# An attention and two-layer feed-forward kernel on one core: value matmuls one item later, weight conversions spread out, PSUM copies divided by size

## The chip, the cores and the metric

The kernel runs on one core of one Trainium2 chip. The metric is the device time of one execution in microseconds. Before the change the median of three runs is 1132.71 us (1131.9 to 1133.64). One further execution was profiled; where the text gives a time of a single instruction, it is from that one.

## The reference

Inputs are `q`, `k`, `v` of 4 batches x 8 heads x 576 positions x 64 in fp32, and four float64 weight matrices (512x2048, 2048x512, twice). What is computed, cut to its core:

```python
q_rot, k_rot = rotate(q), rotate(k)                  # rotary embedding, halves of 32
scores = matmul(q_rot, k_rot.T) / sqrt(64)
attn = exp(scores - max(scores)); attn = attn / (sum(attn) + 1e-9)
x = (attn @ v)   -> 2304 tokens x 512
h = x @ w_in;  g = where(h > 0, h, exp(min(h, 0)) - 1);  x = g @ w_out      # first feed-forward
h = x @ w_in2; g = h - tanh(h);                          out = g @ w_out2   # second
```

## The kernel before

**Attention.** The 32 heads are worked on as 16 pairs. A pair has nine *items*: four blocks of 128 queries for each of its two heads (numbers 0 to 7, the heads in turn) and item 8, which holds the last 64 queries of both. The main loop runs over the 144 items of all pairs, `for i in range(n + D + 1)`, and in iteration i it issues, in this order: the row maximum of item i (`emit_max`, L220, VectorE), the score matmuls of item i+1 (`emit_s`, L211, into one of two PSUM tiles `s`), the exponential of item i (`emit_exp`, L234, ScalarE), the PSUM copies that the iteration before left over (`flush`), the division by the row sum (`emit_norm`, GpSimd), preparation steps of a later pair (`prep`, five steps for each of q and k: two products and a sum for the rotation, a rounded copy, a remainder, then DMAs that put the halves in place), one part of a weight conversion, the transposes of item i-4 (`emit_t`, L291, and the small `pr` ones, into one of three PSUM tiles), and the value matmuls that are due (`emit_pv`, L325).

All engines take their instructions strictly in this order; nothing is reordered at run time. So the place of an instruction in its engine's row decides what stands behind it when it waits. The score tile of item i+2 reuses that of item i, and so waits for the exponential of item i. `flush` deals its copies out in turn: of five, two go to VectorE and three to ScalarE, large (`aT`, 512 columns) or small (`aTr`, up to 128 columns) alike. `PV_AT` says how many iterations after the last transpose of a group its value matmuls are issued: chunks 0 to 2 one later, 3 and 4 three later (the small last group: two).

**Weights.** A weight block (128 x 512, float64) is loaded by `load_w` and turned into two fp32r halves by `conv_w` in NCV = 5 parts: ScalarE `Abs` (L83), two VectorE operations together (L85, L86), one (L90), one (L94), and at the end a ScalarE copy (L102) with a GpSimd subtraction (L103). The work tile `f` has one buffer, so a conversion can't begin until the GpSimd subtraction of the one before it has read `f`. Eight blocks, `first_w`, are converted in attention, one in 18 items.

**Feed-forward.** 192 steps (layer, group of 512 hidden units, one of six blocks of 384 tokens, one of four 128-wide slices). Step i issues `emit_f1(i)` (L445: 12 matmuls), the split of a slice of the next token block's input into two halves (`split_x`: ScalarE copy L54, GpSimd subtraction L55), the split of step i-2's result (`emit_split`), the activation (`emit_act`, L456), its VectorE part (`emit_dve`), conversion parts, and `emit_f2(i-4)` (L503). The four slices of token block 1 are split in steps 0 to 3, and `emit_f1(4)` reads all four.

Of the kernel before, what the change touches and what calls it, by code (L numbers as in the profile page):

```python
# [23 lines left out]
def attention_elu_tanhshrink(ctx: ExitStack, tc: tile.TileContext, qk, v, w1i, w1o, w2i, w2o, tab, out):  # L24
# [14 lines left out]
    NG, NJ = 4, 4  # L39
# [28 lines left out]
        raw_t[key] = t  # L68

    cv_t = {}  # L70
    NCV = 5

    def conv_w(key, slot, part):
        l, kind, c = key
        if part < 4:
            words = raw_t[key].bitcast(U32).rearrange("p (n t) -> p n t", t=2)
            lo_w, hi_w = words[:, :, 0], words[:, :, 1]
        if part == 0:
            cv_t[key] = cv_p.tile([128, 512], F32, tag="f", name="f")
        f = cv_t[key]  # L80
        fu = f.bitcast(U32)
        if part == 0:
            nc.scalar.activation(out=f, in_=hi_w.bitcast(F32), func=AF.Abs)  # L83
        elif part == 1:
            nc.vector.tensor_scalar(out=f, in0=f, scalar1=LO_CLAMP, scalar2=HI_CLAMP, op0=ALU.max, op1=ALU.min)  # L85
            nc.vector.tensor_scalar(  # L86
                out=fu, in0=fu, scalar1=3, scalar2=0x3FFFFFFF, op0=ALU.logical_shift_left, op1=ALU.bitwise_and
            )
        elif part == 2:
            nc.vector.scalar_tensor_tensor(  # L90
                out=fu, in0=hi_w, scalar=0xC0000000, in1=fu, op0=ALU.bitwise_and, op1=ALU.bitwise_or
            )
        elif part == 3:
            nc.vector.scalar_tensor_tensor(  # L94
                out=fu, in0=lo_w, scalar=29, in1=fu, op0=ALU.logical_shift_right, op1=ALU.bitwise_or
            )
            raw_t.pop(key)
        else:
            w = w_pools[slot // 4 if slot < 4 else -1].tile(
                [128, 2, 512], F32R, tag=f"w{kind}_{slot}", name=f"w{kind}_{slot}"  # L100
            )
            nc.scalar.copy(out=w[:, 0, :], in_=f)  # L102
            nc.gpsimd.tensor_tensor(out=w[:, 1, :], in0=f, in1=w[:, 0, :].bitcast(F32), op=ALU.subtract)  # L103
            w_t[key] = w
            cv_t.pop(key)


    with ExitStack() as actx:
# [143 lines left out]
                    out=a, in0=a, scalar1=r[:, x:x + 1], scalar2=1.0, op0=ALU.mult, op1=ALU.mult  # L252
                )

        ev = [0]
        late, late_x = [], []

        def evac(out_, in_):
# [1 line left out]

        def flush():
            for out_, in_ in late:
                ev[0] += 1
                if ev[0] % 5 in (1, 3):
                    nc.vector.tensor_copy(out_, in_)  # L265
                else:
                    nc.scalar.copy(out_, in_)  # L267
            late.clear()
            for p, grp, o, n in late_x:
                b, hp = divmod(p, 4)  # L270
                x0 = NTOK * hp + b * S + 256 * grp
                nc.scalar.copy(out=xa[:, x0:x0 + n], in_=o[:, 0:n])
            late_x.clear()
# [60 lines left out]
        D = 4  # L334
        NDIRECT = 2
        NI = 9
        first_w = [(0, kind, c) for c in range(NJ) for kind in range(2)]
        sched = {}
        early = {1: ((None, 0, 0, 1, 2, 3), (None, 0, 0, 0, 1, 2)), 2: ((0, 4, 5, 7, 7, 8), (4, 7, 9, 11, 12, 13))}
        for p in range(1, NPAIR):  # L340
            i0 = NI * (p - 1)
            for x in range(2):
                when = [i0 + o for o in ((-10, -6, -4, -3, -2, -1), (-7, -2, 0, 2, 3, 4))[x]]
                if p in early:
                    when = early[p][x]
                if when[0] is not None:
                    sched.setdefault(when[0], []).append((load_qk, p, x))
                for k in range(5):
                    sched.setdefault(when[k + 1], []).append((prep, p, x, k))
            sched.setdefault(i0 + 7, []).append((load_v, p))  # L350
        with tc.manual_schedule():
# [17 lines left out]
                prep(0, 1, i)  # L369
            n = len(items)  # L370
            pend = []
            nw = list(range(len(first_w)))[::-1]
            emit_s(0)
            PV_AT = ((1, 1, 1, 3, 3), (1, 1, 1, 3, 3), (2, 2, 2, 2, 2))
            for i in range(3, 5):
                for x in range(2):
                    prep(0, x, i)
            for i in range(n + D + 1):
                p, r = divmod(i, NI)
                for f, *arg in sched.get(i, ()):  # L380
                    if f is not prep:
                        f(*arg)
                if i == 1 or i % (2 * NI) == 12:
                    load_w(first_w[nw.pop()]) if nw else None
                if i < n:
                    emit_max(i)
                if i + 1 < n:
                    emit_s(i + 1)
                if i < n:
                    emit_exp(i)  # L390
                flush()
                if 0 <= i - 1 < n:
                    emit_norm(i - 1)
                if p < NPAIR:
                    for f, *arg in sched.get(i, ()):
                        if f is prep:
                            f(*arg)
                    c = NI * (p % 2) + r - 3
                    if c >= 0 and c % 2 == 0 and c // 2 < NCV and p // 2 < len(first_w):
                        key = first_w[p // 2]  # L400
                        conv_w(key, key[2], c // 2)
                if 0 <= i - D < n:
                    emit_t(i - D)
                    pp, uu, hh = items[i - D]
                    if uu in (1, 3) and hh == 1 or uu == 4:
                        for c in range(5):
                            pend.append((i + PV_AT[uu // 2][c], pp, uu // 2, c))
                for x in [x for x in pend if x[0] <= i]:
                    emit_pv(*x[1:])
                    pend.remove(x)  # L410
                if n - 8 <= i < n and (i - n) % 2 == 0:
                    split_x(0, (i - n + 8) // 2)
# [115 lines left out]
                    nc.sync.dma_start(out=out[128 * r:128 * r + 128, :], in_=a)  # L528

    y_done = []  # L530
    conv = [(l, kind, NJ * g + j) for l in range(2) for g in range(NG) for j in range(NJ) for kind in range(2)]
    conv = conv[2 * NJ:]
    LAG = 4
    with tc.manual_schedule():
        nc.vector.memset(b1, B1)
# [3 lines left out]
        todo = [(key, part) for key in conv for part in range(NCV)]  # L539
        nload = ndone = 0  # L540
        for i in range(n + LAG + 1):
            if i < n:
                emit_f1(i)
            emit_acc()
            if i < NJ * (NT - 1):
                split_x(i // NJ + 1, i % NJ)
            if 0 <= i - 2 < n:
                emit_split(i - 2)
            if i < n:
                emit_act(i)  # L550
            if 0 <= i - 1 < n:
                emit_dve(i - 1)
            while nload < len(conv) and nload <= i // 3:
                load_w(conv[nload])
                nload += 1
            while ndone < len(todo) and ndone < (i - 2) * NCV // 3:
                key, part = todo[ndone]
                ndone += 1
                conv_w(key, key[2] % NJ + NJ * ((key[0] * NG + key[2] // NJ) % 2), part)
            if 0 <= i - LAG < n:  # L560
                emit_f2(i - LAG)
# [57 lines left out]
```

## Time and profile before

| what | value |
|---|---|
| median of the runs | 1132.71 us |
| profiled execution | 1132.65 us, of it the span 1130.9 us |
| TensorE matmul busy | 1097.3 us (97%) |
| VectorE busy | 765.6 us (68%) |
| ScalarE busy | 688.6 us (61%) |
| GpSimd busy | 671.3 us (59%) |

The span falls into a start up to about 24 us, attention up to about 319 us, and feed-forward after it. Engines in rows: PE is TensorE's matmul, PEld its weight load, DVE is VectorE, ACT ScalarE, POOL GpSimd, SP the engine that issues the DMAs. A matmul's row can be longer than its share of the engine, since matmuls overlap; the distance of starts tells the pace. A name before the arrow is written, those behind it are read.

### The profile page before, as it was taken

To read this page: it belongs to the slowest core of one execution; us is meant where nothing else is said; L and a number is where in the kernel's file an instruction comes from. 1 tells how busy PE (TensorE), PEld (TensorE's weight loads), DVE (VectorE), ACT (ScalarE), POOL (GpSimd) and SP (SyncE) were. 2 spreads that over 40 slices of the span, in tenths; PEclk is the share of its full clock that TensorE was granted. 3 is DMA by queue.
4 is the path that set the end of the run, shared out by engine and by line. 5 is a ranking of instruction groups with operands and counts; after the bars stand their busy time and mean duration, and the time that the engine had idled before them with its cause. 6 is when DMAs were issued, how large, how long until landed. Compare 5 with 4: busy or idle time off the path is not lost.

```text
span 1130.9 us, 18518 instructions
## 1 busy us (share of the span) xinstructions
PE 1097.3 (97%) x6656; PEld 987.2 (87%) x6656; DVE 765.6 (68%) x1393; ACT 688.6 (61%) x1477; POOL 671.3 (59%) x609
## 2 busy tenths in 40 slices
PE   2899999999999999999999999999999999999998
PEld 2777776777799999999999999998998899899987
DVE  6988888888645434555545556678768877877665
ACT  3676766676745533333333344688888788877774
POOL 2877887887556533333333466676666666666443
PEclk9999999999999999999999999999999999999999
DMA  7767676865211111112111121111111111110102
GB/s 232 217 193 200 181 215 169 222 172 164 72 39 38 40 55 38 38 38 55 40 38 38 38 57 38 39 38 38 57 38 38 38 56 38 38 39 1 57 35 78
DMA packets 29627, 91.96 MB, mean 81 GB/s; under 512 B 4192, under 2 KB 4192, under 8 KB 29536
## 3 DMA queue, kind: packets, MB, share of 16 engines
q1 hardware_dynamic: 29536, 90.78, 28.3%
q8 instruction: 53, 0.87, 0.3%
q14 instruction: 38, 0.31, 0.1%
HBM read 57.74 MB, written 4.72 MB: 55 GB/s over the span
## 4 chain that ended last, share of the span: by engine, by line
PE 90%; DVE 5%; DMA 2%; ACT 2%; SPq 1%; issue 1%; ACTq 0%; DVEq 0%
PE h L445 36%; PE y L503 18%; PE y L505 17%; PE o L325 8%; PE s L211 6%; PE pt L291 4%; DVE nm L220 2%; DMA k<-hl 1%; ACT a L234 1%; DVE t L148 1%; DVE aT L265 1%; ACT aT L267 1%; DVE hl L156 0%; DMA tabs<-in_tab 0%; PE pr L304 0%
## 5 line engine op out<-in xcount | busy, mean ns | idle before, releaser
L445 PE MATMUL h<-x,w 128*128 128x384 f32 x2304 | 434.0, 336 | 0.0
L445 PEld LDWEIGHTS h<-x,w 128*128 128x128 f32 x2304 | 407.1, 188 | 8.0 <-ACT a L234 0.4
L488 POOL TENSOR_TENSOR g<-f,g 128x384 fp32r<-128x384 f32 x192 | 213.6, 1113 | 187.8 <-ACT g L487 182.5
L503 PE MATMUL y<-g,w 128*128 128x384 f32 x1152 | 219.0, 339 | 0.0
L505 PE MATMUL y<-w,g 128*128 128x512 f32 x864 | 216.7, 395 | 0.2 <-ACT xa L520 0.2
L503 PEld LDWEIGHTS y<-g,w 128*128 128x128 f32 x1152 | 204.0, 188 | 0.0
L505 PEld LDWEIGHTS y<-w,g 128*128 128x128 f32 x864 | 161.5, 188 | 31.9 <-ACT xa L520 0.6
L251 POOL TENSOR_SCALAR a<-a,r 128x576 f32<-128x576 f32 x144 | 135.2, 951 | 63.7 <-DVE r L248 43.6
L464 POOL TENSOR_TENSOR w<-w,u 128x384 f32<-128x384 f32 x96 | 105.4, 1098 | 99.7 <-ACT w L463 99.7
L234 ACT ACTIVATE a<-s,nm 128x576 f32<-128x576 f32 x144 | 107.1, 743 | 89.6 <-DVE nm L220 75.1
L487 ACT CAST g<-f 128x384 fp32r<-128x384 f32 x192 | 98.0, 510 | 94.1 <-PE y L503 92.4
L475 DVE TENSOR_SCALAR f<-f 128x384 f32<-128x384 f32 x96 | 40.0, 416 | 145.4 <-ACT f L456 145.4
L456 ACT ACTIVATE f<-h 128x384 f32<-128x384 f32 x96 | 47.2, 492 | 146.7 <-PE h L445 143.8
L220 DVE TENSOR_REDUCE nm<-s 128x1 f32<-128x576 f32 x144 | 108.2, 753 | 38.1 <-PE s L211 36.5
L103 POOL TENSOR_TENSOR w<-f,w 128x512 fp32r<-128x512 f32 x64 | 82.6, 1291 | 54.4 <-ACT w L102 54.3
L522 DVE TENSOR_TENSOR xa<-y,xa 128x384 f32<-128x384 f32 (+1 forms) x126 | 74.0, 612 | 47.3 <-PE y L503 42.0
L479 DVE TENSOR_TENSOR f<-h,f 128x384 f32<-128x384 f32 x96 | 53.1, 553 | 68.3 <-ACT f L465 67.8
L481 DVE COPY_PREDICATED f<-mask,w 128x384 f32<-128x384 uint32 x96 | 92.2, 961 | 10.3 <-DVE w L480 0.5
L325 PE MATMUL o<-aT,v 128*64 128x256 f32 (+1 forms) x768 | 89.3, 339 | 2.6 <-ACT aT L267 2.4
L146 POOL TENSOR_TENSOR t<-t,tabs 128x576 f32<-128x576 f32 x59 | 86.3, 1463 | 8.2 <-DMA t<-in_qk 8.2
L291 PE MATMUL pt<-ident,a 128*128 128x128 f32 x576 | 88.3, 277 | 0.1
L461 ACT ACTIVATE u<-h 128x384 f32<-128x384 f32 x96 | 47.4, 494 | 66.4 <-PE h L445 52.1
(55 smaller groups left out, 1379.2 us busy)
## 6 DMA issues: line engine op xcount, KB each, us to landing
k<-hl SPq DMA_DIRECT2D x64, 288.0 KB, 4.2
t<-in_qk SPq DMA_DIRECT2D x30, 576.0 KB, 6.2
raw<-in_w1i SPq DMA_DIRECT2D x16, 512.0 KB, 3.7
raw<-in_w1o SPq DMA_DIRECT2D x16, 512.0 KB, 3.7
raw<-in_w2i SPq DMA_DIRECT2D x16, 512.0 KB, 3.6
raw<-in_w2o SPq DMA_DIRECT2D x16, 512.0 KB, 3.6
v<-in_v SPq DMA_DIRECT2D x16, 288.0 KB, 4.7
qa<-hl SPq DMA_DIRECT2D x32, 144.0 KB, 4.0
```

What stands on the lines that cost most here:

```text
L220: nc.vector.tensor_reduce(out=nm, in_=s_t[i][:, :, 0:288], axis=AX.XY, op=ALU.max, negate=True)
L234: nc.scalar.activation(out=a.rearrange("p (x c) -> p x c", x=2), in_=s[:, :, 0:288], func=AF.Exp, bias=nm_t.pop(i), scale=1.0, accum_out=den,)
L251: nc.gpsimd.tensor_scalar(out=a, in0=a, scalar1=r[:, x:x + 1], scalar2=1.0, op0=ALU.mult, op1=ALU.mult)
L291: nc.tensor.transpose(pt[:, c, :], a[:, h or 0, c0:c0 + 128], ident)
L325: nc.tensor.matmul(out=o[sl, 0:n], lhsT=w, rhs=m, start=(c == 0), stop=(c == 4))
L445: nc.tensor.matmul(out=hp, lhsT=w[:, wp, ws], rhs=x_t[t][:, xp, c, :], start=(m == 0), stop=(m == 3 * KC - 1))
L464: nc.gpsimd.tensor_tensor(out=w, in0=w, in1=u, op=ALU.mult)
L481: nc.vector.copy_predicated(f, mask.bitcast(U32), w)
L487: nc.scalar.copy(out=g[:, 0, :], in_=f)
L488: nc.gpsimd.tensor_tensor(out=g[:, 1, :], in0=f, in1=g[:, 0, :].bitcast(F32), op=ALU.subtract)
L503: nc.tensor.matmul(out=y_t[e][:, 0:NB], lhsT=w[:, wp, es], rhs=gt[:, gp, :], start=st, stop=sp)
L505: nc.tensor.matmul(out=y_t[e], lhsT=gt[:, gp, es], rhs=w[:, wp, :], start=st, stop=sp)
```

## The change

Three things change. The value matmuls are due one iteration later (`PV_AT`). `flush` gives every copy of at most 128 columns to VectorE and every larger one to ScalarE. The weight conversions are cut into NCV = 6 parts (L85 and L86 apart) and spread: one block takes 28 items, with its parts at offsets `CV_AT`, so that five blocks (`NFIRST`) instead of eight are converted in attention; the other three, which are the `w_out` blocks of the first group's slices 1 to 3, are converted whole in steps 0, 1 and 2 of feed-forward, and their loads stand on SP's queue behind attention's last. Preparation steps move by up to one iteration. From step 3 on, feed-forward converts one block in three steps, as before.

```diff
-    NCV = 5
+    NCV = 6
...
         elif part == 1:
             nc.vector.tensor_scalar(out=f, in0=f, scalar1=LO_CLAMP, scalar2=HI_CLAMP, op0=ALU.max, op1=ALU.min)
+        elif part == 2:
             nc.vector.tensor_scalar(
                 out=fu, in0=fu, scalar1=3, scalar2=0x3FFFFFFF, op0=ALU.logical_shift_left, op1=ALU.bitwise_and
             )
...
+    conv = [(0, kind, c) for kind in range(2) for c in range(NJ)]
+    conv += [(l, kind, NJ * g + j) for l in range(2) for g in range(NG) for j in range(NJ) for kind in range(2)][2 * NJ:]
+    NFIRST = NJ + 1
...
         def flush():
             for out_, in_ in late:
-                ev[0] += 1
-                if ev[0] % 5 in (1, 3):
+                if out_.free_size() <= 128:
                     nc.vector.tensor_copy(out_, in_)
                 else:
                     nc.scalar.copy(out_, in_)
...
-        first_w = [(0, kind, c) for c in range(NJ) for kind in range(2)]
+        CYC, CV_AT = 28, (5, 8, 12, 17, 21, 24)
...
-                when = [i0 + o for o in ((-10, -6, -4, -3, -2, -1), (-7, -2, 0, 2, 3, 4))[x]]
+                when = [i0 + o for o in ((-10, -7, -6, -4, -3, -2), (-7, -2, -1, 1, 2, 3))[x]]
...
-            PV_AT = ((1, 1, 1, 3, 3), (1, 1, 1, 3, 3), (2, 2, 2, 2, 2))
+            PV_AT = ((2, 2, 2, 4, 4), (2, 2, 2, 4, 4), (3, 3, 3, 3, 3))
...
-                if i == 1 or i % (2 * NI) == 12:
-                    load_w(first_w[nw.pop()]) if nw else None
+                key, at = divmod(i, CYC)
+                key = conv[key] if key < NFIRST else None
+                if key and at == 0:
+                    load_w(key)
...
-                    c = NI * (p % 2) + r - 3
-                    if c >= 0 and c % 2 == 0 and c // 2 < NCV and p // 2 < len(first_w):
-                        key = first_w[p // 2]
-                        conv_w(key, key[2], c // 2)
+                    if key and at in CV_AT:
+                        conv_w(key, key[2], CV_AT.index(at))
...
-    conv = conv[2 * NJ:]
+    conv = conv[NFIRST:]
...
-            while nload < len(conv) and nload <= i // 3:
-                load_w(conv[nload])
-                nload += 1
-            while ndone < len(todo) and ndone < (i - 2) * NCV // 3:
+            upto = NCV * min(i + 1, 2 * NJ - NFIRST) + max(0, (i - 2) * NCV // 3)
+            while ndone < min(len(todo), upto):
+                while nload < len(conv) and nload <= ndone // NCV + 1:
+                    load_w(conv[nload])
+                    nload += 1
                 key, part = todo[ndone]
```

On TensorE, around item 8 of the first full pair (the `s` row with 224 columns belongs to it), the row of instructions before was:

```order
L211 MATMUL s<-k_197,qa_97 128x288 x4
L211 MATMUL s<-k_200,qb_99 128x288 x2
L211 MATMUL s<-k_200,qb_99 128x224 x2
L211 MATMUL s<-k_200,qb_99 128x64 x2
L291 MATMUL pt<-ident,a 128x128 x4
L304 MATMUL pr<-ident,a 128x128
L211 MATMUL s<-k_479,qa_96 128x288 x4
L291 MATMUL pt<-ident,a 128x128 x4
L325 MATMUL o<-aT,v 64x256 x6
L211 MATMUL s<-k_482,qb_98 128x288 x4
```

and now, at the same place (line numbers are those of the changed file):

```order
L217 MATMUL s<-k_197,qa_97 128x288 x4
L217 MATMUL s<-k_200,qb_99 128x288 x2
L217 MATMUL s<-k_200,qb_99 128x224 x2
L217 MATMUL s<-k_200,qb_99 128x64 x2
L295 MATMUL pt<-ident,a 128x128 x4
L308 MATMUL pr<-ident,a 128x128
L217 MATMUL s<-k_466,qa_96 128x288 x4
L295 MATMUL pt<-ident,a 128x128 x4
L217 MATMUL s<-k_469,qb_98 128x288 x4
L295 MATMUL pt<-ident,a 128x128 x4
L308 MATMUL pr<-ident,a 128x128
L329 MATMUL o<-aT,v 64x256 x6
```

The value matmuls `o` stood between item 8's scores and those of the second item after it; they now stand behind these.

On ScalarE, from the first activation of feed-forward on (`x_4304` is token block 1, `f<-h` the activation, `f<-raw` the start of a conversion and `w<-f` its end), the row before was:

```order
L456 ACTIVATE f<-h 128x384
L54 CAST x_4304<-xa 128x384
L456 ACTIVATE f<-h 128x384
L54 CAST x_4304<-xa 128x384
L487 CAST g<-f 128x384
L456 ACTIVATE f<-h 128x384
L54 CAST x_4304<-xa 128x384
L487 CAST g<-f 128x384
L456 ACTIVATE f<-h 128x384
L83 ACTIVATE f<-raw 128x512
```

and now, from the instruction behind the first activation on (`x_4271` is token block 1):

```order
L83 ACTIVATE f<-raw 128x512
L103 CAST w_1_4311<-f 128x512
L54 CAST x_4271<-xa 128x384
L460 ACTIVATE f<-h 128x384
L83 ACTIVATE f<-raw 128x512
L103 CAST w_2_4341<-f 128x512
L54 CAST x_4271<-xa 128x384
L491 CAST g<-f 128x384
L460 ACTIVATE f<-h 128x384
L83 ACTIVATE f<-raw 128x512
L103 CAST w_3_4374<-f 128x512
L54 CAST x_4271<-xa 128x384
```

The last three splits of token block 1 stand behind one, two and three whole conversions, where before they stood behind none.

On VectorE, from iteration 5 of attention on (`nm` is a row maximum, `f` the conversion), the row before was:

```order
L220 TENSOR_REDUCE nm<-s 128x1
L265 COPY aT<-pt 128x4x128
L85 TENSOR_SCALAR f<-f 128x512
L86 TENSOR_SCALAR f<-f 128x512
L220 TENSOR_REDUCE nm<-s 128x1
L265 COPY aTr<-pr 128x128
L247 TENSOR_SCALAR den<-den 128x1 x2
L248 RECIPROCAL r<-den 128x2
L220 TENSOR_REDUCE nm<-s 128x1
```

and now:

```order
L226 TENSOR_REDUCE nm<-s 128x1 x2
L269 COPY aTr<-pr 128x128
L253 TENSOR_SCALAR den<-den 128x1 x2
L254 RECIPROCAL r<-den 128x2
L226 TENSOR_REDUCE nm<-s 128x1
L154 TENSOR_TENSOR t_150<-t_150 128x576
L226 TENSOR_REDUCE nm<-s 128x1
```

A large copy and two parts of a conversion no longer stand between two row maxima.

## Rows read from the trace of the kernel before

**Rows 1.** Stages: length; busy us of PE, PEld, DVE, ACT, POOL; clock, DMA, GB/s.

```profile
51.00:304.00 253.00, 247.02 (x2042) 187.56 (x2041) 212.68 (x480) 175.83 (x441) 200.83 (x187) 1.00 0.68 183
...
319.00:1131.00 812.00, 807.92 (x4317) 768.23 (x4315) 510.74 (x832) 482.71 (x967) 437.42 (x388) 1.00 0.14 42
```

**Rows 2.** TensorE's waits on large copies: us in total, times, longest.

```profile
PE pr L297 <- ACT aT L267: 3.0, 3, 1.2
PE o L325 <- ACT aT L267: 2.4, 4, 1.4
```

**Rows 3.** Timeline, TensorE: last value matmuls of pairs 0, 13, 14; start, duration.

```profile
50.81 0.69 PE L325 MATMUL o<-aT,v 128*64 128x64 f32 x16
...
286.87 0.69 PE L325 MATMUL o<-aT,v 128*64 128x64 f32 x16
...
304.32 0.69 PE L325 MATMUL o<-aT,v 128*64 128x64 f32 x16
```

**Rows 4.** Timeline behind item 8 of pair 13; in brackets idle time and releaser.

```profile
273.32 0.74 ACT L234 ACTIVATE a<-s,nm 128x576 f32<-128x576 f32 x1 [0.20 <-DVE nm L220]
...
273.98 0.19 PEld L325 LDWEIGHTS o<-aT,v 128*64 128x64 f32 x2 [0.17 <-issue]
...
274.68 1.05 PEld L325 LDWEIGHTS o<-aT,v 128*64 128x64 f32 x10 [0.51 <-ACT aT L267]
```

**Rows 5.** Timeline of the start of attention.

```profile
33.20 0.74 ACT L234 ACTIVATE a<-s,nm 128x576 f32<-128x576 f32 x1 [3.47 <-DVE nm L220]
...
34.08 0.80 PE L211 MATMUL s<-k,qa 128*128 128x288 f32 x4 [3.04 <-ACT a L234]
...
37.35 1.80 POOL L146 TENSOR_TENSOR t<-t,tabs 128x576 f32<-128x576 f32 x1 [1.09 <-DMA t<-in_qk]
...
39.13 2.62 POOL L251 TENSOR_SCALAR a<-a,r 128x576 f32<-128x576 f32 x3
...
41.77 0.60 PE L291 MATMUL pt<-ident,a 128*128 128x128 f32 x4
```

**Rows 6.** Stages behind that wait; columns as in rows 1.

```profile
34.00:40.00 6.00, 5.92 (x35) 4.71 (x35) 5.51 (x13) 4.92 (x12) 4.91 (x4) 0.72 0.91 301
36.00:38.00 2.00, 2.00 (x11) 1.84 (x9) 1.84 (x7) 1.61 (x4) 0.91 (x2) 0.50 1.03 417
```

**Rows 7.** Timeline of the start of feed-forward.

```profile
318.64 10.15 PE L445 MATMUL h<-x,w 128*128 128x384 f32 x57
...
320.50 0.49 ACT L456 ACTIVATE f<-h 128x384 f32<-128x384 f32 x1 [0.91 <-PE h L445]
...
325.05 0.50 ACT L54 CAST x<-xa 128x384 fp32r<-128x384 f32 x1
...
325.64 1.01 POOL L55 TENSOR_TENSOR x<-xa,x 128x384 fp32r<-128x384 f32 x1
...
328.63 2.28 PE L503 MATMUL y<-g,w 128*128 128x384 f32 x12
```

**Rows 8.** The conversion's operations by line: duration ns min/median/max, first and last start.

```profile
L83 ACT ACTIVATE f<-raw x64: 652/668/687, 27.2 to 1022.8; 128x512 f32<-128x512 f32 x64
...
L85 DVE TENSOR_SCALAR f<-f x64: 402/534/1642, 29.6 to 1024.3; 128x512 f32<-128x512 f32 x64
...
L86 DVE TENSOR_SCALAR f<-f x64: 426/428/1506, 30.9 to 1025.6; 128x512 uint32<-128x512 uint32 x64
...
L90 DVE SCALAR_TENSOR_TENSOR f<-raw,f x64: 679/693/1781, 35.0 to 1026.0; 128x512 uint32<-128x512 uint32 x64
...
L94 DVE SCALAR_TENSOR_TENSOR f<-raw,f x64: 664/681/1512, 38.7 to 1029.0; 128x512 uint32<-128x512 uint32 x64
...
L102 ACT CAST w<-f x64: 605/613/663, 44.5 to 1031.2; 128x512 fp32r<-128x512 f32 x64
...
L103 POOL TENSOR_TENSOR w<-f,w x64: 1267/1292/1305, 45.2 to 1031.9; 128x512 fp32r<-128x512 f32 x64
```

**Rows 9.** DMA issues: KB each, median us from issue to landing.

```profile
raw<-in_w1o SPq DMA_DIRECT2D x16, 512.0 KB, 3.7
```

More of the change, by code (lines that the diff above doesn't have):

```diff
@@ L70, in attention_elu_tanhshrink @@
     cv_t = {}
-    NCV = 5
+    NCV = 6
     def conv_w(key, slot, part):
         l, kind, c = key
-        if part < 4:
+        if part < 5:
             words = raw_t[key].bitcast(U32).rearrange("p (n t) -> p n t", t=2)
@@ L88, in conv_w @@
             )
-        elif part == 2:
+        elif part == 3:
             nc.vector.scalar_tensor_tensor(
@@ L92, in conv_w @@
             )
-        elif part == 3:
+        elif part == 4:
             nc.vector.scalar_tensor_tensor(
@@ L253, in emit_norm @@
                 )
-        ev = [0]
         late, late_x = [], []
@@ L371, in attention_elu_tanhshrink @@
             pend = []
-            nw = list(range(len(first_w)))[::-1]
             emit_s(0)
-            PV_AT = ((1, 1, 1, 3, 3), (1, 1, 1, 3, 3), (2, 2, 2, 2, 2))
+            PV_AT = ((2, 2, 2, 4, 4), (2, 2, 2, 4, 4), (3, 3, 3, 3, 3))
             for i in range(3, 5):
@@ L530, in attention_elu_tanhshrink @@
     y_done = []
-    conv = [(l, kind, NJ * g + j) for l in range(2) for g in range(NG) for j in range(NJ) for kind in range(2)]
-    conv = conv[2 * NJ:]
+    conv = conv[NFIRST:]
     LAG = 4
```

## The prediction

> **What bounds the kernel now.** I read the busy times by stage first. In feed-forward TensorE is busy 807.9 of 812 us, in the pairs of attention 247.0 of 253 [rows 1]. So feed-forward is as long as its matmuls, and only its beginning can change; in attention there is little idle time, but a long row of a matmul can hide a wait. So I took the pace from the timeline. From the last value matmuls of pair 0 to those of pair 14 there are 14 pairs in 304.32 - 50.81 = 253.5 us, 18.1 us each; the last of them took 304.32 - 286.87 = 17.45 us [rows 3]. The same matmuls are in each pair, so a pair needs 17.45 us or less. I put its floor at 17.23, an estimate, since that pair is hardly free of waits itself. What is above the floor, 253.5 - 14 x 17.23 = 12.3 us (with a floor of 17.45: 9.2), is all that removed waits can give back there. The list of waits names part of it: TensorE waiting for large copies on ScalarE, 3.0 + 2.4 us, up to 1.2 and 1.4 at once [rows 2]. The rest is score matmuls behind an exponential whose row maximum came late on VectorE.
>
> The Trainium skill, "Perfetto Trace Analysis", section "Identifying the Most-Contended Engine", says that TensorE's headroom is to be judged by its weight loads' busy share, not by that of the matmuls. By that share 253 - 187.6 = 65 us would be spare in attention [rows 1]; by the pace of the pairs 12.3 us are [rows 3]. I go by the pace, since a pair at the floor has the same loads.
>
> **The start of attention: 1.6 us less.** VectorE does a large copy and L85 and L86 between the row maxima of items 5 and 6. TensorE then waits 3.04 us for the exponential at 33.20 [rows 5], and soon after runs at the lower clock: from 36 to 38 us 0.50 was granted, which is 1.2 instead of 2.4 GHz, and 0.72 in the mean from 34 to 40 [rows 6]. The change takes all three operations out of there. But the next wait stands close behind: GpSimd waits for a load of the third pair's k until 37.35, multiplies it for 1.80 us and only then, at 39.13, divides items 6, 7 and 8, three in 2.62 us or 0.87 each [rows 5]. The transposes of item 6 need the first of these, so they can't begin before 39.13 + 0.87 + 0.1 = 40.1, where they now begin at 41.77. The loads in front are on SP's queue in the same order, so I keep 37.35. The gain is 41.7 - 40.1 = 1.6 us. Bounds: 0, and 3.0 for the wait plus what the low clock cost, (1 - 0.72) x 6 = 1.7 us [rows 6], together 4.7.
>
> **The pairs: 12.3 us of waits go, 6.9 come.** The value matmuls now stand an iteration behind the copy that they need, and VectorE loses 40% of the large copies; I let all 12.3 us of old waits go. But the value matmuls also were what TensorE did between item 8's scores and those of two items later, which reuse item 8's score tile. Now only transposes and one item's scores stand there. In pair 13 the exponential of item 8 starts at 273.32 [rows 4], and from its start to the scores that wait for one are 34.08 - 33.20 = 0.88 us [rows 5], so these can start at 274.20. TensorE would have reached them at 273.98 - 0.17 = 273.81, where the weight load of the value matmuls was due behind the transposes [rows 4]. That is a new wait of 0.39 us, in every pair, whatever the other engines do: 15 x 0.39 = 5.9 us. Behind the waiting scores stand the next transposes and all of that group's value matmuls. Of the 20 conversion operations on VectorE (four of each of five blocks), twelve fall into iterations that already hold a preparation step. Most of these have value matmuls on TensorE beside them, which cover a row maximum that is 0.43 to 0.69 us late [rows 8]; I count four without that cover at 0.25 us, 1.0 us (bounds 0, and 12 x 0.69 = 8.3). Sum for the pairs: -12.3 + 5.9 + 1.0 = -5.4 us.
>
> The 40% of the nine large copies of a pair that move to ScalarE cost nothing by themselves: its small copies leave, it has 253 - 175.8 = 77 us to spare, over 5 a pair [rows 1], and the matmuls cover them. Preparation one iteration earlier, with its DMAs now in front of or behind a load of v on SP, is hidden by nine items for q and five for k. If that cover failed it would show as the wait for DMAs in the start does.
>
> **The end of attention: 0.9 us more.** There are no scores left there to stand between the transposes of item 4 of the last pair and those of item 5, which need the tile that ScalarE copies after item 8's exponential. In the row of pair 13 that copy freed its reader at 274.68, and the transposes of item 4 were through at the same 273.81 [rows 4]: 0.87 us. The value matmuls that filled this are now behind it. Bounds 0 and 1.
>
> **The start of feed-forward: 9.7 us more.** Let T be the start of the long row of f1 matmuls, 318.64 before [rows 7]. f1(4) needs all four slices of token block 1. Before, the last is cast at 325.05 and its second half is ready at 325.64 + 1.01 = 326.65, T + 8.0; f1(4) is through when f2(0) starts, at 328.63, T + 10.0 [rows 7]. Now three whole conversions stand in front of that cast on ScalarE. A conversion is a chain over three engines: 0.67 + (0.53 + 0.43 + 0.69 + 0.68) + 0.61 + 1.29 = 4.9 us of medians [rows 8]; with four hand-overs of 0.09, as from the cast (325.05 + 0.50) to GpSimd (325.64) [rows 7], 5.3. ScalarE can't take anything else in between, since its next instruction is the end of the same conversion, and the `Abs` after it waits for GpSimd to have read the one work tile. The first conversion begins behind the first activation, at T + 1.86 + 0.49 = T + 2.35 [rows 7]. Two whole ones: T + 12.9. The third up to its ScalarE copy, 3.6 + 3 x 0.09 = 3.9: T + 16.8. The cast of the last slice: T + 17.3. GpSimd meanwhile ends the third conversion at T + 18.1 and then needs 1.0 for the slice's second half: T + 19.2. Three of f1(4)'s matmuls use that slice, and two come after its second half, at 10.15 / 57 = 0.18 us each [rows 7]: f1(4) ends at T + 19.65 instead of T + 10.0, 9.7 us later. Behind f1(4) on TensorE stand f2(0) and everything else, and feed-forward has no idle time in which to make it good. f2(0) to f2(3) find their inputs ready by then.
>
> Bounds: with the shortest durations, 4.7 a conversion [rows 8], and ScalarE's instructions overlapping a little, 8.9. In the third conversion VectorE works while GpSimd subtracts; L86 and L90 went up to 1.51 and 1.78 us [rows 8], which would add 1.1 each: 11.9. The load of the second block uses a buffer in attention's space, is issued at about T and lands 3.7 us later [rows 9], before its conversion at T + 7.6; that of the third waits for L94 of the first, at about T + 5.4, and lands before T + 12.9. The Trainium skill, "SBUF — State Buffer", section "Who interferes with whom", has VectorE operations with two SBUF inputs block for a whole GpSimd instruction. By that rule L90 and L94 of the third conversion would lose up to 1.3 us each and the sum would be up to 2.6 us higher; the medians of rows 8 lie at the bottom of their spread, so I don't take it.
>
> **The clock after it: 1.7 us more.** During those 9.7 us TensorE does only a few matmuls. After the 3.04 us wait in attention the clock fell, and that cost the 1.7 us above [rows 5, 6]; I take the same here. Bounds 0 and twice that, 3.4.
>
> **Sum.** -1.6 - 5.4 + 0.9 + 9.7 + 1.7 = +5.3. The profiled execution took 1132.65 us, of them 1130.9 the span, so 1137.95; the median of the runs, 1132.71, is as good as the same. I predict 1138 us, its own range 1134 to 1142.
>
> **Rivals.** *Faster: attention gives all.* The old waits go, the new one at item 8 is covered because its exponential comes earlier on a relieved VectorE, and no clock is lost: -12.3 - 1.6 + 0.9 + 8.9 = -4.1, 1128.5 us. For it: VectorE is the busier engine, 212.7 of 253 us [rows 1]. The Trainium skill, "Perfetto Trace Analysis", section "Optimizing Scalar/DVE Operations", advises to offload a saturated VectorE to ScalarE. Against it: between item 8's scores and its exponential only the row maximum and two hand-overs are left, which a freer VectorE doesn't shorten. It decides as soon as the new wait is under 0.1 us. Chance 0.15. *Faster: the three conversions hide.* Only if f1(4) didn't need its slices so late: -1.6 - 5.4 + 0.9, 1126.5 us; the order on ScalarE speaks against it. 0.04. *The two sides cancel*: the chain costs 8.9, the pairs give 9, the clock nothing, the start 1.6, with the end's 0.9 1131.9, and up to 1134 with less from the pairs. 0.17. *Slower still: ScalarE sets the pace*, since each iteration's large copy stands behind its exponential and before the next. If pr or transposes then wait 0.5 us more in each of 15 pairs, 7.5 us more: 1145. Against it: ScalarE is at 70% [rows 1]. 0.10. The forecast has 0.54.
>
> A change of 0.2% (2.3 us) is what a measurement of this kernel can tell from none. Faster than that: 0.15 + 0.04 = 0.19. Within: the cancelling case, 0.17. Slower: 0.54 + 0.10 = 0.64. The range 1129.5 to 1143.5 leaves out about half of the faster and of the slowest case.
>
> **What would show it.** After: pairs at 17.5 to 17.9 us; a wait of scores for ScalarE of about 0.4 us behind item 8 in each pair, and none of value matmuls for a copy; f2(0) starting some 19.7 us after f1's long row began, with f1(4) waiting for GpSimd's slices; a stretch of clock 0.50 there, and none near 36 us. I am wrong if the slices of token block 1 come earlier than that, or if pairs stay at 18.1 us.

## The result

The changed kernel took 1145.68 us (median of four runs, 1145.15 to 1147.21), the kernel before 1132.81 (1131.90 to 1133.64): a ratio of 1.0116, interval 1.0098 to 1.0134. It is slower, as forecast, but by 12.9 us where 5.3 were predicted, and 1145.7 lies above the range. The profiled execution took 1145.54 us, of them 1143.8 the span.

The stages, with the columns of [rows 1]:

```profile
53.00:306.00 253.00, 245.16 (x2020) 184.63 (x2018) 190.00 (x460) 186.78 (x440) 192.17 (x184) 1.00 0.64 176
34.00:40.00 6.00, 4.62 (x37) 3.54 (x36) 3.42 (x9) 4.39 (x10) 3.06 (x4) 1.00 0.97 318
...
330.00:344.00 14.00, 8.16 (x23) 6.85 (x24) 10.03 (x15) 6.62 (x15) 10.38 (x9) 0.51 0.28 76
346.00:1143.00 797.00, 793.74 (x4234) 753.80 (x4232) 490.40 (x816) 474.70 (x950) 415.49 (x378) 1.00 0.13 42
```

VectorE is 22.7 us less busy in 253 us of pairs, ScalarE 11 us more, and the fall of the clock near 36 us [rows 6] is gone. A new one stands at 330 to 344 us. TensorE's waits (total, times, longest):

```profile
PE s L217 <- ACT a L240: 8.6, 21, 2.0
...
PE h L449 <- ACT x L54: 5.4, 2, 2.9
PE h L449 <- POOL x L55: 2.4, 2, 1.2
```

The waits of value matmuls for copies [rows 2] are gone; scores now wait for exponentials, and f1 for slices. The timeline of TensorE where attention ends, against [rows 7]:

```profile
318.90 9.12 PE L449 MATMUL h<-x,w 128*128 128x384 f32 x51
330.50 0.69 PE L449 MATMUL h<-x,w 128*128 128x384 f32 x1 [2.48 <-ACT x L54]
332.39 1.01 PE L449 MATMUL h<-x,w 128*128 128x384 f32 x2 [1.21 <-POOL x L55]
336.33 0.69 PE L449 MATMUL h<-x,w 128*128 128x384 f32 x1 [2.94 <-ACT x L54]
338.22 1.01 PE L449 MATMUL h<-x,w 128*128 128x384 f32 x2 [1.20 <-POOL x L55]
339.03 4.04 PE L507 MATMUL y<-g,w 128*128 128x384 f32 x12
```

The long f1 row begins at 318.90 instead of 318.64: attention gives nothing. f2(0) begins 20.13 us behind it instead of 9.99, which is 10.1 us, and its twelve matmuls take 4.04 instead of 2.28 us at the lower clock; by 345.39, where f2(1) begins (332.85 before), another 2.1 us are lost. These two make 12.3 of the 12.9.

In attention, the pairs. The last value matmuls of pairs 0 and 14, as in [rows 3]:

```profile
51.29 0.69 PE L329 MATMUL o<-aT,v 128*64 128x64 f32 x16
...
306.13 0.69 PE L329 MATMUL o<-aT,v 128*64 128x64 f32 x16
```

14 pairs take 254.84 us, 18.2 each; before 253.5. The new wait is there: between two pairs with little else to wait for, the scores of the second item behind item 8 start at 93.33 and 111.08, 17.75 us apart, each behind 0.39 us of an idle weight loader. The matmuls lose less than the loader idles: their own row shows 0.15 us idle there.

```profile
93.33 0.56 PEld L217 LDWEIGHTS s<-k,qb 128*128 128x128 f32 x4 [0.39 <-ACT a L240]
...
111.08 0.56 PEld L217 LDWEIGHTS s<-k,qb 128*128 128x128 f32 x4 [0.39 <-ACT a L240]
```

```profile
93.33 0.79 PE L217 MATMUL s<-k,qb 128*128 128x288 f32 x4 [0.15 <-ACT a L240]
```

A pair in which TensorE waits for nothing else takes 17.59 us, from one last row of value matmuls to the next:

```profile
216.18 0.69 PE L329 MATMUL o<-aT,v 128*64 128x64 f32 x16
...
233.77 0.69 PE L329 MATMUL o<-aT,v 128*64 128x64 f32 x16
```

What wasn't foreseen stands at 67.63, TensorE's largest wait in the pairs. VectorE before it, and GpSimd beside it:

```profile
62.23 1.93 DVE L162 SCALAR_TENSOR_TENSOR hl<-t,hl 128x576 fp32r<-128x576 f32 x1 [0.85 <-ACT hl L157]
64.09 1.90 DVE L95 SCALAR_TENSOR_TENSOR f<-raw,f 128x512 uint32<-128x512 uint32 x1
65.91 0.74 DVE L226 TENSOR_REDUCE nm<-s 128x1 f32<-128x576 f32 x1
```

```profile
62.13 3.30 POOL L152 TENSOR_TENSOR t<-t,tabs 128x576 f32<-128x576 f32 x2
```

```profile
67.63 0.79 PE L217 MATMUL s<-k,qa 128*128 128x288 f32 x4 [1.97 <-ACT a L240]
```

A preparation's remainder and a conversion part, 0.76 and 0.68 us when nothing is beside them, take 1.93 and 1.90 us beside two products on GpSimd, and the row maximum behind them is 2.4 us late. At 267.33 the same happens (1.52 us), with L85 as the conversion part, 1.63 us long. The remainders and the products in the pairs, before and now (busy us, mean ns, idle before):

```profile
L156 DVE SCALAR_TENSOR_TENSOR hl<-t,hl 128x576 fp32r<-128x576 f32 x26 | 26.0, 1001 | 4.3 <-ACT hl L151 2.9 <-DMA t<-in_qk 0.6
...
L146 POOL TENSOR_TENSOR t<-t,tabs 128x576 f32<-128x576 f32 x50 | 72.1, 1442 | 0.0
```

```profile
L162 DVE SCALAR_TENSOR_TENSOR hl<-t,hl 128x576 fp32r<-128x576 f32 x25 | 32.2, 1288 | 19.5 <-ACT hl L157 17.8 <-DMA k<-hl 1.7
...
L152 POOL TENSOR_TENSOR t<-t,tabs 128x576 f32<-128x576 f32 x50 | 82.8, 1665 | 0.0
```

Both sides pay: a product takes 1.67 instead of 1.44 us.

### The profile page after: what moved, and what is told of

Read it like the earlier page. It is cut to its first block, busy times and chain, and to the rows that moved or that the text cites. A ratio compares the mean times of both kernels' runs of the same rounds, so it can differ in the third digit from the quotient of the medians.

```text
span 1143.8 us, 18511 instructions
## 1 busy us (share of the span) xinstructions
PE 1101.0 (96%) x6656; PEld 987.7 (86%) x6656; DVE 734.4 (64%) x1383; ACT 705.8 (62%) x1487; POOL 655.2 (57%) x609
## 4 chain that ended last, share of the span: by engine, by line
PE 83%; DVE 7%; POOL 3%; ACT 3%; issue 2%; DMA 1%; SPq 1%; ACTq 0%; POOLq 0%; DVEq 0%
PE h L449 34%; PE y L507 18%; PE y L509 17%; PE s L217 6%; PE o L329 6%; PE pt L295 3%; DVE nm L226 2%; DVE hl L162 2%; POOL t L152 1%; DVE t L154 1%; ACT a L240 1%; POOL a L257 1%; DVE f L95 1%; ACT hl L157 0%; POOL x L55 0%
## 5 line engine op out<-in xcount | busy, mean ns | idle before, releaser
L492 POOL TENSOR_TENSOR g<-f,g 128x384 fp32r<-128x384 f32 x192 | 206.8, 1078 | 198.0 <-ACT g L491 194.8
L468 POOL TENSOR_TENSOR w<-w,u 128x384 f32<-128x384 f32 x96 | 101.5, 1057 | 103.0 <-ACT w L467 103.0
L257 POOL TENSOR_SCALAR a<-a,r 128x576 f32<-128x576 f32 x144 | 118.5, 834 | 71.9 <-DVE r L254 70.3
L85 DVE TENSOR_SCALAR f<-f 128x512 f32<-128x512 f32 x64 | 29.5, 461 | 172.5 <-ACT f L83 172.5
L152 POOL TENSOR_TENSOR t<-t,tabs 128x576 f32<-128x576 f32 x59 | 96.6, 1648 | 10.0 <-DMA t<-in_qk 10.0
L526 DVE TENSOR_TENSOR xa<-y,xa 128x384 f32<-128x384 f32 (+1 forms) x126 | 72.5, 610 | 23.5 <-PE y L507 18.3
L271 ACT COPY aT<-pt 128x512 f32<-128x512 f32 x144 | 83.5, 582 | 1.8 <-PE pt L295 1.8
L329 PE MATMUL o<-aT,v 128*64 128x256 f32 (+1 forms) x768 | 80.1, 337 | 0.0
```

What stands on the lines that cost most here:

```text
L152: eng.tensor_tensor(out=t[:, i, :], in0=t[:, i, :], in1=tabs[:, i, :], op=ALU.mult)
L257: nc.gpsimd.tensor_scalar(out=a, in0=a, scalar1=r[:, x:x + 1], scalar2=1.0, op0=ALU.mult, op1=ALU.mult)
L329: nc.tensor.matmul(out=o[sl, 0:n], lhsT=w, rhs=m, start=(c == 0), stop=(c == 4))
L468: nc.gpsimd.tensor_tensor(out=w, in0=w, in1=u, op=ALU.mult)
L492: nc.gpsimd.tensor_tensor(out=g[:, 1, :], in0=f, in1=g[:, 0, :].bitcast(F32), op=ALU.subtract)
```

## The experiments

Two theories. For feed-forward: three whole conversions ahead of the slices of token block 1. For attention: two of the change's edits, the preparation one item earlier and the conversions in 28 items, put VectorE's SBUF operations beside GpSimd's products and behind each other, and that eats what later value matmuls and copies by size would give. All edits are to the changed kernel if not said otherwise. "First f1" is the start of the three f1 matmuls that stand near attention's end (309.41 before, 310.14 changed); "to f2(0)" is the time from there to f2(0) (19.2 before, 28.9 changed). Three of the kernels have the same attention to the instruction (the changed one and the two with three parts a step); their first f1 comes at 310.14, 310.58 and 309.61, and their 14 pairs take 254.84, 255.29 and 254.75 us. So differences of first f1 under 1 us and of the pairs under 0.6 us say nothing.

| run | median us | ratio to before, interval | first f1 | to f2(0) |
|---|---|---|---|---|
| eight in attention | 1128.20 | 0.9969 (0.9956 to 0.9981) | 305.12 | 18.7 |
| three parts a step | 1149.97 | 1.0161 (1.0147 to 1.0175) | 310.58 | 21.4 |
| old preparation | 1140.38 | 1.0076 (1.0063 to 1.0089) | 305.49 | 28.9 |
| values as before | 1159.25 | 1.0243 (1.0229 to 1.0257) | 324.02 | 29.4 |
| before, values later | 1133.69 | 1.0016 (1.0007 to 1.0025) | 310.69 | 18.7 |
| before, copies by size | 1135.22 | 1.0028 (1.0017 to 1.0039) | 312.20 | 19.2 |
| three parts, old pace | 1141.55 | 1.0084 (1.0071 to 1.0098) | 309.61 | 21.4 |
| eight, old preparation | 1132.63 | 1.0003 (0.9995 to 1.0012) | 308.68 | 18.7 |
| five in eighteen | 1140.60 | 1.0076 (1.0064 to 1.0089) | 305.98 | 28.9 |
| no products | 1135.45 | 1.0033 (1.0020 to 1.0045) | 299.56 | 28.9 |
| values spread | 1170.40 | 1.0348 (1.0324 to 1.0373) | 358.59 | 14.0 |
| clear of preparation | 1131.71 | 0.9993 (0.9984 to 1.0002) | 308.89 | 18.7 |

**Eight blocks in attention.**

```
-    NFIRST = NJ + 1
+    NFIRST = 2 * NJ
...
-        CYC, CV_AT = 28, (5, 8, 12, 17, 21, 24)
+        CYC, CV_AT = 18, (3, 5, 8, 11, 13, 15)
```

> The changed kernel, but all eight first weight blocks are converted within attention again (one per 18 items, its six parts at items 3, 5, 8, 11, 13, 15), and none at the start of feed-forward. Theory A (three whole conversions on ScalarE in front of token block 1's last slice cost 10.1 us, and the low clock behind them 2.1): f2(0) starts 10 us after f1's long row began, no stretch of clock 0.50 there, and with about 1 us more of collisions in attention (32 conversion operations on VectorE instead of 20) the time is 1145.7 - 12.3 + 1 = 1134.5 us, between 1133 and 1137. Rival B (the slices come late for another reason, as the preparation moved one item earlier or the copies by size): f2(0) still starts 17 us or more after the row began, 1143 us or more.

1128.2: theory A for feed-forward, and 5.0 us of attention besides, where 1 us more of collisions was expected. VectorE at the place of the 1.97 us wait:

```profile
62.91 1.93 DVE L162 SCALAR_TENSOR_TENSOR hl<-t,hl 128x576 fp32r<-128x576 f32 x1 [0.85 <-ACT hl L157]
64.76 0.74 DVE L226 TENSOR_REDUCE nm<-s 128x1 f32<-128x576 f32 x1
```

The remainder is as slow, but no conversion part is behind it, and TensorE's matmuls don't wait there.

**Five blocks at those items.** The edit above without NFIRST.

> The changed kernel with its five blocks in attention and three at the start of feed-forward, but the five stand at the items of the run with eight blocks (one per 18 items, parts at items 3, 5, 8, 11, 13, 15), where only one VectorE part falls into an iteration with a preparation step on VectorE, instead of 10 of 20 in the changed kernel's 28 items. Theory A (5.0 us of attention are lost because a conversion part on VectorE stands behind a preparation step there, both slowed beside GpSimd's product, so that the row maximum behind them is late): the first f1 comes at 305 to 306 us instead of 310.1, the waits of 2.04 and 1.59 us are gone, the start of feed-forward costs what it cost in the changed kernel, 1140 to 1141.5 us. Rival B (eight blocks in attention shorten it for another reason, as fewer splits at its end): 1144 us or more.

As A said. Against the changed kernel this moves only the five blocks' parts: 310.14 - 305.98 = 4.2 us of attention. The gain in the pairs is larger, as this execution reached the end of pair 0 later (52.86 instead of 51.29): 14 pairs take 249.1 instead of 254.84 us, 5.7 less.

```profile
52.86 0.69 PE L329 MATMUL o<-aT,v 128*64 128x64 f32 x16
...
301.96 0.69 PE L329 MATMUL o<-aT,v 128*64 128x64 f32 x16
```

Against the run of eight it moves only three blocks to feed-forward: 1140.6 - 1128.2 = 12.4 us, of which 0.9 lies ahead of the first f1.

**The old preparation items.**

```
-                when = [i0 + o for o in ((-10, -7, -6, -4, -3, -2), (-7, -2, -1, 1, 2, 3))[x]]
+                when = [i0 + o for o in ((-10, -6, -4, -3, -2, -1), (-7, -2, 0, 2, 3, 4))[x]]
```

> The changed kernel, but the preparation of the next pair's q and k stands at the items of before again (offsets -6, -4, -3, -2, -1 and -2, 0, 2, 3, 4). Theory A (the preparation's remainders on VectorE now begin beside a product on GpSimd, 23 of 25 of them instead of 5 of 26, and take a median of 1.01 and up to 1.96 us instead of 0.76; with the conversion parts that collide in the same way they make the late row maxima): L162 is back at a median of 0.76, the waits of 2.04 and 1.59 us of scores at 67.6 and 267.3 are gone or under 0.5, and attention is 3 to 5 us shorter: 1141 to 1143 us. Rival B (the waits come from where the conversions stand, and the remainders are covered): attention within 1.5 us of the changed kernel's, 1144.5 us or more.

(The first number of each row is the load. One step, q's second product, moved by two items and not by one; and q's remainder stood in the changed kernel in the same item as k's first product, both at -2, where now they are an item apart.) A, a little more than it said. The remainders and the products in the pairs:

```profile
L162 DVE SCALAR_TENSOR_TENSOR hl<-t,hl 128x576 fp32r<-128x576 f32 x26 | 21.5, 826 | 2.5 <-ACT hl L157 1.6
...
L152 POOL TENSOR_TENSOR t<-t,tabs 128x576 f32<-128x576 f32 x50 | 72.0, 1441 | 0.0
```

14 pairs take 250.3 us, 4.5 less than in the changed kernel:

```profile
51.16 0.69 PE L329 MATMUL o<-aT,v 128*64 128x64 f32 x16
...
301.47 0.69 PE L329 MATMUL o<-aT,v 128*64 128x64 f32 x16
```

The items alone don't keep the two apart: the kernel before has the same ones, and there the remainders' mean was 1.00 us, with 10 of 26 beside a product; here it is 1 of 26.

**No products on GpSimd.**

```
+                    if p >= 2:
+                        return
                     eng = nc.vector if p < 2 and i == 1 else nc.gpsimd
```

> The changed kernel, leaving out the table products of the preparation on GpSimd from the third pair on (so the scores of those pairs are of untabled q and k); every VectorE, ScalarE and TensorE instruction stays where it is. Theory A (VectorE's operations on SBUF take up to 1.9 us because GpSimd reads and writes SBUF beside them): the remainders take 0.76 us and the conversion parts 0.41 and 0.68 in all places, the waits at 67.6 and 267.3 are gone, attention 4 to 5 us shorter, 1140.5 to 1142 us. Rival B (the operations are slow for another reason, as ScalarE's or the DMAs' use of SBUF): they stay at 1.6 to 1.9 us here and there, and the time is within 1.5 us of the changed kernel's.

A again, and more than it said: attention is 10.6 us shorter, not 4 to 5. VectorE's operations in the pairs, and the last value matmuls of pairs 0 and 14:

```profile
L164 DVE SCALAR_TENSOR_TENSOR hl<-t,hl 128x576 fp32r<-128x576 f32 x25 | 19.8, 792 | 17.8 <-ACT hl L159 17.8
L95 DVE SCALAR_TENSOR_TENSOR f<-raw,f 128x512 uint32<-128x512 uint32 x5 | 3.6, 719 | 0.0
...
L85 DVE TENSOR_SCALAR f<-f 128x512 f32<-128x512 f32 x4 | 1.7, 413 | 0.0
```

```profile
49.31 0.69 PE L331 MATMUL o<-aT,v 128*64 128x64 f32 x16
...
295.54 0.69 PE L331 MATMUL o<-aT,v 128*64 128x64 f32 x16
```

246.2 us, 17.59 a pair in the mean, as long as the changed kernel's own quickest pair above: the wait behind item 8 and no other that matters, with all conversions and preparations on VectorE and ScalarE where they were. Pair 1, between the scores of item 8 of pairs 0 and 1, takes 18.9 instead of 20.9 us. How much of the 10.6 us is slowed VectorE and how much GpSimd's own time (sums no longer wait for products, and divisions no longer stand behind them) this run doesn't part. The products were not left out of the kernel before, so how much of its own waits they made is open.

**Three parts a step at the start of feed-forward.**

```
-upto = NCV * min(i + 1, 2 * NJ - NFIRST) + max(0, (i - 2) * NCV // 3)
+upto = min(3 * (i + 1), NCV * (2 * NJ - NFIRST)) + max(0, (i - 5) * NCV // 3)
```

> The changed kernel, but the three conversions at the start of feed-forward are issued three parts at a time over steps 0 to 5 instead of six at a time over steps 0 to 2; the same work, in the same place of the program. Theory A (what costs is that a whole conversion is one chain through ScalarE, VectorE, GpSimd and back, behind which the slice splits stand): only one of the three chains' two halves stands ahead of each slice, the cast of the last slice follows one whole conversion and one Abs, f2(0) starts 10 to 13 us after the long row began, and the time is 1133.5 to 1137 us. Rival B (the amount of work there is what costs, as 3 x 1.3 us of ScalarE, 3 x 2.3 of VectorE and 3 x 1.3 of GpSimd must be done beside the slices whatever their order): half or more of the 12.3 us stays, 1139 us or more.

f2(0) comes 7.5 us earlier, as A says, yet the run is slower: the edit also put all later blocks three steps later, and from 733 us on f1 waits for its weights (4.9 + 2.9 us in the list, in four places).

> The changed kernel, with the three conversions issued three parts at a time over steps 0 to 5 as in the earlier run, but the later blocks at the changed kernel's pace again (that run had shifted them by three steps, and f1 then waited for weights at 733, 838, 942 and 1047 us, 1.4 + 0.9 us each and more in the second layer). Theory A (chains in front of the slices): f2(0) starts 21.4 us after the first f1 as in that run (28.9 in the changed kernel, 19.2 before), no low clock, no waits for weights later, 1145.7 - 7.5 - 2.1 = 1136 us, between 1134.5 and 1137.5. Rival B: as the blocks of steps 3 to 5 get five parts in a step, the waits come back one step later: 1139 us or more.

B here: 1141.5, not 1136. With (i - 2) again the start is the same, but three steps of five parts follow, and TensorE waits for GpSimd there:

```profile
345.01 2.03 PE L507 MATMUL y<-g,w 128*128 128x384 f32 x10 [0.82 <-POOL g L492]
...
349.27 0.79 PE L449 MATMUL h<-x,w 128*128 128x384 f32 x3 [1.01 <-POOL x L55]
351.49 0.62 PE L449 MATMUL h<-x,w 128*128 128x384 f32 x2 [1.43 <-POOL x L55]
```

So the order of the chains makes 7.5 of the 9.7 us to f2(0), but the three blocks have no free place in the first steps: only 1145.7 - 1141.5 = 4.2 us of the whole time come back. The profiled execution took 1139.4, the other four 1141.5; what these two more are is open.

**Values as before; and each alone on the kernel before.**

```
-PV_AT = ((2, 2, 2, 4, 4), (2, 2, 2, 4, 4), (3, 3, 3, 3, 3))
+PV_AT = ((1, 1, 1, 3, 3), (1, 1, 1, 3, 3), (2, 2, 2, 2, 2))
```

> The changed kernel, but the value matmuls stand at the items of before again. Theory A (the value matmuls one item later make the wait of 0.40 us behind item 8 in each pair, 15 x 0.4 = 6 us, and save the waits for copies of about 5.4): the 0.40 waits go, waits of value matmuls for ScalarE's large copies come back, and since all large copies now stand behind an exponential on ScalarE they are not smaller than before: between 1144 and 1147 us, the same as the changed kernel within 0.15%. Rival B (the new wait is the larger): 1140 us or less. Rival C (the later value matmuls hide much more than 6 us now that ScalarE does all large copies): 1150 us or more.

C, which I hadn't believed. The waits of value matmuls come back, 19 of them:

```profile
PE o L329 <- ACT aT L271: 10.6, 19, 1.1
```

> The kernel before, with the value matmuls one item later and nothing else changed. Theory A (they shed the waits for copies, 5.4 us in the list, and make the wait behind item 8, 15 x 0.4 = 6 us, and 0.9 at attention's end; late row maxima stay): the pairs within 3 us of before's, between 1130 and 1136 us. Rival B (the later value matmuls are what saves: without them the changed kernel was 13.6 us slower): 1122 to 1128 us. Rival C (they only pay beside the copies by size): 1136 us or more.

A. The wait behind item 8 is in this run too, with nothing else changed:

```profile
55.99 0.56 PEld L211 LDWEIGHTS s<-k,qb 128*128 128x128 f32 x4 [0.39 <-ACT a L234]
```

Besides, TensorE waits three times in the pairs for the DMAs that put k and q in place, which it does nowhere in the pairs of before or of the changed kernel:

```profile
PE s L211 <- DMA k<-hl: 2.5, 2, 1.6
PE s L211 <- DMA qa<-hl: 1.2, 1, 1.2
```

So with later value matmuls the earlier preparation has a use: the changed kernel has no such wait in its pairs, and with the old preparation items it has two of 0.4 us.

> The kernel before, with all large copies on ScalarE and all small ones on VectorE and nothing else changed. Theory A (a large copy on ScalarE stands behind an exponential, so with value matmuls one item behind their copy they wait some 0.8 us twice in a pair, as in the kernel without the later value matmuls, 1159 us; of its 27 us beyond before, 12.3 belong to feed-forward): 1140 to 1147 us, waits of value matmuls for ScalarE's copies 20 us or more in the list. Rival B (VectorE is relieved of 40% of the large copies, and what waits is covered): 1127 to 1133 us, and the waits of 36 us go.

(`if ev[0] % 5 in (1, 3):` becomes `if out_.free_size() <= 128:`.) Neither: 1135.2. The pairs become even, 18.3 us each; the weight loader waits twice in a pair for a copy, 0.69 and 0.3 us. So the edits are not a sum: alone, values cost 1.9 us and copies 3.5; values are worth 13.6 where the copies and the slowed remainders are there too.

**Eight blocks and the old preparation.** Both edits.

> The changed kernel with all eight blocks converted in attention (as in the run of 1128.2 us) and also the old items of preparation (the run of 1140.4 us, 5.3 us less than the changed kernel). Theory A (a remainder slowed beside GpSimd's products costs only where a conversion part falls beside it too; one per 18 items never does that): the two gains overlap, and the time is within 1.5 us of 1128.2. Rival B (each slowed remainder costs by itself): 1123 to 1126 us.

Both theories miss: 1132.6, 4.4 us worse than eight blocks with the new items. With the old items conversion parts at items 8, 11 and 13 fall into iterations with a preparation step on VectorE again, and scores wait in every second pair (at 85.86 us behind a remainder of 1.07 and a conversion part of 0.68; the loader idles 0.79 us, the matmuls 0.55), so that this needs hardly any slowing by GpSimd.

```profile
85.86 0.80 PE L217 MATMUL s<-k,qb 128*128 128x288 f32 x4 [0.55 <-ACT a L240]
```

Neither preparation is better by itself; it depends on where the conversions stand.

**Clear of preparation.** Eight blocks, `CV_AT` (4, 6, 8, 11, 13, 15), the first block at (4, 6, 9, 10, 12, 15).

> The kernel with eight blocks in attention (1128.2 us), with each block's parts at items 4, 6, 8, 11, 13, 15 of its 18 (the first block's at 4, 6, 9, 10, 12, 15), so that no conversion part on VectorE falls into an iteration with a preparation step there, also not in the first two pairs, where three still did. Theory A (only such pairs of operations cost): the waits at 44.75 (1.11 us), 49.91 (0.76) and 102.6 (0.32) go, 1126 us, between 1125.3 and 1127.3. Rival B (what is left in the first pairs comes from the loads of k and q there): 1127.6 us or more.

A fails: 1131.7, 3.5 us worse. The first pairs kept their waits, and in every second pair the scores now wait at the place of 68.68 us, as ScalarE has the moved first part in front of the exponential:

```profile
67.20 0.70 ACT L83 ACTIVATE f<-raw 128x512 f32<-128x512 f32 x1
67.80 0.74 ACT L240 ACTIVATE a<-s,nm 128x576 f32<-128x576 f32 x1
```

```profile
68.68 0.80 PE L217 MATMUL s<-k,qb 128*128 128x288 f32 x4 [0.45 <-ACT a L240]
```

One item earlier the same 0.70 us cost nothing: there TensorE has value matmuls between those scores and the ones before.

**Values spread,** on the run of eight: `PV_AT` ((3, 3, 3, 5, 5), (2, 2, 2, 6, 6), (5, 5, 5, 5, 5)).

> The kernel with eight blocks in attention (1128.2 us), and the value matmuls placed so that some stand again between item 8's scores and those of two items later: the first group's three and five items behind, the second group's last two row groups six, the third group's five. Theory A (the 0.40 us wait behind item 8 is nothing but TensorE having no work there): the 15 waits go, 15 x 0.4 = 6 us less, pairs of 17.3 to 17.4 us, 1122.5 us. Rival B (the next pair's value matmuls find the one o tile still being copied, or other scores wait instead): the 0.4 us come back at another place, pairs of 17.7 us or more, 1127.5 us or more.

B: the value matmuls do find the one o tile not yet copied, but for a reason that B didn't have. The load of v waits for the value matmuls of the pair two before, which are now later, and holds SP's queue: it goes out at 56.79 instead of 53.22, and the load of the weights behind it at 61.41 instead of 57.14. ScalarE then stands before the conversion, and the copy of o stands behind it (seven such waits of value matmuls, 21.9 us in all):

```profile
66.63 0.67 ACT L83 ACTIVATE f<-raw 128x512 f32<-128x512 f32 x1 [3.13 <-DMA raw<-in_w1i]
...
68.38 0.38 ACT L276 COPY xa<-o 128x256 f32<-128x256 f32 x1
```

```profile
68.81 1.55 PE L329 MATMUL o<-aT,v 128*64 128x256 f32 x6 [3.54 <-ACT xa L276]
```

Whether the wait behind item 8 can be filled stays open.

## Why the prediction was wrong

- **The start of feed-forward, +9.7: right.** 10.1, with the chain and the order on ScalarE as worked out; the run of eight blocks takes it away.
- **The clock, +1.7: right.** 2.1. Together 12.3 by the timeline, and 12.4 by the two runs that differ in these blocks alone, of which 0.9 belongs to attention.
- **The start of attention, -1.6, and the low clock there:** the scores of item 8 of pair 0 come 2.8 us earlier and the clock stays at 1.00, but pair 1, up to its own item 8, takes 20.9 instead of 18.6 us, so that a gain of 0.5 is left, no more than the scatter named above.
- **The pairs, -12.3 + 5.9 + 1.0 = -5.4: the step that failed, and in it the third term.** Measured is 254.8 - 253.5 = +1.3: the pairs stay at 18.2 us, the sign of being wrong that the prediction named. The third term, conversion parts beside preparation steps, was 1.0 with bounds to 8.3. Moving the conversions' places alone (five in eighteen) gives back 5.7 us of the pairs, moving the preparation alone 4.5, and leaving out the products 254.8 - 246.2 = 8.6; the first two break up the same meetings and don't add: together, with eight blocks, they make a slower kernel than the first with eight blocks. I had sized the term with free durations (0.43 to 0.69 us); beside GpSimd's products the operations take up to 1.9 us. Those long durations were in [rows 8] as maxima, and I put them aside. I had also called the preparation one iteration earlier hidden, having looked only at its inputs and not at what runs beside it. The count of twelve was wrong too: by the order of issue nine of the 20 operations stand in an iteration with a preparation step on VectorE.
- **The first two terms in it, -12.3 + 5.9:** right in their sum, by luck. The pace that they give is 17.23 + 0.39 = 17.62 us a pair; an undisturbed pair takes 17.59. But the 17.45 us pair of [rows 3], which I called hardly free of waits, shows no wait of TensorE's matmuls in the trace, so 9.2 us could be given back and not 12.3; and a pair with the new wait is only 17.59 - 17.45 = 0.14 us longer than that one, 2.0 in 14 pairs and not 5.9. Both were too large by 3 to 4 us.
- **The end of attention, +0.9:** -0.6, from item 8 of the last pair to the long f1 row (11.0 instead of 11.57 us). The kernel before with later values alone has the same -0.6, so it belongs to that edit; I had looked for a loss and missed a gain.

The Trainium skill, "SBUF — State Buffer", section "Who interferes with whom", from which VectorE operations with two SBUF inputs block for a whole GpSimd instruction, was named in the prediction and not taken. The runs bear it out: the remainder takes 1.93 us where it starts beside a product and a mean of 0.79 in the run without them. The forecast's sign came from feed-forward alone. "The two sides cancel" needed the pairs to give what they did not.

## What to carry to other kernels

Where a schedule moves work of VectorE, look up what GpSimd does at the new place, and where VectorE and GpSimd both work on SBUF at the same time, size an operation by the maximum of its durations and not by its median. An edit's price depends on the others (later value matmuls cost 1.9 us alone and saved 13.6 in the changed kernel; the earlier preparation cost 5.3 us there and saved 4.4 beside eight blocks), so measure pairs of them. The quickest version found keeps the change and converts all eight blocks in attention, 18 items each: 1128.2 us, 0.31% less than before (interval 0.19 to 0.44%).

## What the hardware showed unexpectedly

VectorE's row maxima, which read PSUM, keep their time beside GpSimd's products (medians in the pairs 0.747 us beside one and 0.743 without), while its operations from SBUF to SBUF go up to 1.9 us, those with one input too (in the pairs L85 once beside a product, 1.63 us, else 0.41). GpSimd loses too: a product takes 1.67 us in the mean instead of 1.44. And between 330 and 344 us, with TensorE busy 8.2 of 14, the granted clock stood at 0.51, which is 1.2 of 2.4 GHz, also for the last 5 us of it, in which TensorE had no more pauses.
